# Output weights of layer one kept as halves, and three blocks of layer two split ahead of the seam

## The chip, the cores and the metric

The kernel runs on one core of a Trainium2 chip. TensorE (PE) does the matmuls, VectorE (DVE), ScalarE (ACT) and GpSimd (POOL) the rest, and every DMA is issued by SyncE (SP), on one hardware queue. The metric is the device time in microseconds; the median of three runs of the kernel before is 956.66 us (956.12 to 958.75).

## The reference

Banded causal attention with a distance bias, and on its output two feed-forward layers, all in float32. There are 4 x 576 = 2304 tokens of width 512. The weights come as float64.

```python
scores = where(0 <= rel < 128, q @ k.T / 8 + bias, -1e9)   # 4 batches, 8 heads, 64 wide
x = softmax(scores) @ v                                     # [2304, 512]
g = x @ w_gate; x = (g * sigmoid(g) * (x @ w_val)) @ w_out  # layer one, d_ff 1536
h = x @ w_in
y = (h * tanh(softplus(h))) @ w_out2                        # layer two, d_ff 2048
```

## The kernel before, in words

**Halves.** A float32 operand is split into a high part in the matmul's format (ACT copies it, `hi_act`) and the remainder (DVE subtracts, `lo_dve`). These are its halves. A product of two split operands is three matmuls: high by high, high by low, low by high.

**Weights.** The float64 bits are turned into float32 on the chip by five steps on ACT and DVE (`convert`), and then split (`halves`).

**Attention and layer one** run in five chunks of 384 or 512 tokens (`A_CHUNKS`). While PE does layer one of chunk c, the attention of chunk c+1 is mixed in. The last chunk has no attention beside it. For each of 12 blocks of the hidden width there is a gate and a value group (24 matmuls together, `gv_groups`) and an output group of 12 matmuls (`out_group`). The output weights come in six "rings", r = 0 to 5, each for two output groups, in two SBUF buffers (`ring_tile`). In chunk 0 a ring is converted, its float32 form is written to DRAM (`w1od`, 0.5 MB each) and it is split. In chunks 1 to 4 it is loaded back (`load_ring`, tile `cw`) and split again: one ACT and one DVE instruction on 128x1024 elements. In the last chunk the output groups lag by six, so that groups 5 to 11 stand on PE back to back at its end.

**Layer two** uses seven block products in place of eight. Each of its 16 blocks of input weights (8 used per pass over the tokens, three passes of 768 tokens) is made from a float32 block `w2d` by four differences on POOL (tile `t4`) and a split of seven parts on ACT and DVE (`make_win`, tile `win`, three buffers). Its output weights go through the same steps before the seam (`combos`), and are stored in DRAM as halves (`w2o`). The float32 blocks `w2d` are converted in the stretches of chunks 1 to 3 (`conv_w2`).

**The seam** is the end of the last chunk of layer one and the start of layer two. Behind the last gate and value group PE has output groups 5 to 11, and then `hidden(0, 0)`, `hidden(0, 1)` and so on, 42 matmuls each. `layer2` issues the first loads and the splits of the tokens (`x_parts`) while those output groups run.

**Order.** PE runs in the order in which the code is written (`manual_schedule`). The order on the other engines and on SP is set by the scheduler. Small steps of conversion work wait in a list `bg`, from which `pump` takes some after each PE group. SP issues in order: a DMA that waits for a semaphore holds up all behind it.

Of the kernel before, what the change touches and what calls it, by code (L numbers as in the profile page):

```python
# [27 lines left out]
TB = 384  # L28
NPB = NT // (2 * TB)
NJ = NF2 // 2  # L30

SLOT = {1: 0, 2: 1, 3: 2, 5: 3, 6: 4, 7: 5, 4: 6}
CFG = dict(
# [59 lines left out]
def body(ctx: ExitStack, tc: tile.TileContext, qT, kT, vP, w1, w1o, w2, cst, yT):  # L93
# [7 lines left out]
    ps = ctx.enter_context(tc.tile_pool(name="ps", bufs=4, space=bass.MemoryType.PSUM))  # L101

    x2d = dr.tile([128, CT, NT], F32, name="x2d")
    w1od = dr.tile([NF1 // 2, 128, 1024], F32, name="w1od")
    w2d = dr.tile([NF2, 128, 1024], F32, name="w2d")
    w2o = dr.tile([7, 128, NJ, 2, 256], F32, name="w2o")
    cst_sb = const.tile([128, 452], F32, name="cst_sb")
    nb = {128: cst_sb[:, 0:128], 0: cst_sb[:, 128:256]}
    ident = cst_sb[:, 256:384]
# [298 lines left out]
    def steps(key, fs, front=False):  # L408
        if front:
            bg.extendleft([(key if f is fs[-1] else None, f) for f in fs][::-1])  # L410
            return
        for f in fs[:-1]:
            bg.append((None, f))
        bg.append((key, fs[-1]))
# [36 lines left out]
    def halves(st, alloc, put):  # L451
        def f1():
            st["h"] = alloc()
            hi_act(st["h"][:, 0], st["w"])

        def f2():
            lo_dve(st["h"][:, 1], st["w"], st["h"][:, 0])
            put(st["h"])

        return [f1, f2]  # L460
# [28 lines left out]
    def conv_ring(r):  # L489
        st = {}  # L490

        def spill_it():
            nc.sync.dma_start(out=w1od[r], in_=st["w"])

        def put(w):
            ring[0, r] = w
            stage.pop(("o", r))
            if r + 1 < NF1 // 2:
                stage_other(("o", r + 1), w1o[r + 1])

        steps(
            ("ring", 0, r),
            convert(stage["o", r], st) + [spill_it] + halves(st, ring_tile, put),
        )

    def load_ring(ci, r):
        st = {}

        def f0():
            st["w"] = hp_.tile([128, 1024], F32, tag="cw", name="cw")  # L510
            nc.sync.dma_start(out=st["w"], in_=w1od[r])

        def put(w):
            ring[ci, r] = w

        steps(
            ("ring", ci, r), [f0, lambda: None] + halves(st, ring_tile, put), True
        )

    def conv_w2(blocks, calls):  # L520

        pause = max(6, (calls - 24 - 9 * len(blocks)) // len(blocks))

        def wait(n):
            for _ in range(n):
                bg.append((None, lambda: None))

        def block(i, after):
            st, raw = {}, {}

            def run(k):
                if not raw:
                    raw["f"] = convert(stage.pop(("2", i)), st)
                raw["f"][k]()

            def put():
                nc.sync.dma_start(out=w2d[i], in_=st["w"])

            for k in (0, 2, 3):
                bg.append((None, lambda k=k: run(k)))  # L540
                wait(1)
            if after is not None:
                bg.append((None, lambda: stage_other(("2", after), w2[after])))
            bg.append((None, lambda: run(1)))
            bg.append((None, lambda: run(4)))
            bg.append((None, put))
            wait(pause)

        bg.append((None, lambda: stage_other(("2", blocks[0]), w2[blocks[0]])))
        wait(pause)  # L550
        for i, after in zip(blocks, blocks[1:] + [None]):
            block(i, after)

    def differences(w, x):
        for o, a, b in ((0, w[:, 0], w[:, 1]), (1, w[:, 3], x[:, 0]), (2, w[:, 3], w[:, 0]), (3, x[:, 1], w[:, 2])):
# [247 lines left out]
    def layer2(br):  # L803
# [7 lines left out]
        raws = {}  # L811

        def load_raw(p, j):
            raws[p, j] = br.tile([128, 4, 256], F32, tag="w4", name="w4", bufs=2)
            nc.sync.dma_start(out=raws[p, j], in_=w2d[j].rearrange("p (k n) -> p k n", k=4))

        def make_win(p, j):

            w = raws.pop((p, j))
            x = t4  # L820
            for o, a, b in ((0, w[:, 0], w[:, 1]), (1, w[:, 3], x[:, 0]), (2, w[:, 3], w[:, 0]), (3, x[:, 1], w[:, 2])):
                nc.gpsimd.tensor_tensor(out=x[:, o], in0=a, in1=b, op=ALU.subtract)  # L822
            t = win[p, j] = br.tile([128, 2, 7, 256], F32R, tag="win", name="win")
            for d, src in ((slice(0, 3), w[:, 1:4]), (slice(3, 7), x)):
                hi_act(t[:, 0, d], src)
                lo_dve(t[:, 1, d], src, t[:, 0, d])
# [47 lines left out]
                if i == 7:  # L874
                    add(g[:, 2], g[:, 1], g[:, 0], ALU.subtract)

        load_raw(0, 0)
        t4 = br.tile([128, 4, 256], F32, tag="t4", name="t4", bufs=1)
        xs = x_tiles(br, (7, 5))
        xr = first["x"]  # L880
        xs.update(x_tiles(br, (1, 4, 6, 2, 3)))
        load_raw(0, 1)
        x_parts(xs, xr)
        for j in range(2):
            make_win(0, j)
            load_raw(0, j + 2)
        bp, mish = yield
        yr = yT.rearrange("(c p) t -> p c t", p=128)
        for p in range(NPB):
            loads = [(i, k) for i in ORDER2 for k in range(2)]  # L890
            for j in range(NJ):
                for f, k in ((make_win, p * NJ + j + 2), (load_raw, p * NJ + j + 4)):
                    if k < NPB * NJ:
                        f(*divmod(k, NJ))
                if j >= NJ - 3:
                    load_wout(p, *loads.pop(0))
                hidden(p, j, xs)
# [61 lines left out]
    with tc.manual_schedule(engines={mybir.EngineType.PE}):  # L959
# [28 lines left out]
        while at < lasts[0]:  # L988
            pieces.popleft()[2]()
            at += 1  # L990
            if at == 1:
                conv_w1(0)
                conv_ring(0)
                conv_w1(1)
                nst = len(bg)
                stage_w1(2)
                stage_w1(3)
            f = (at / lasts[0] - CFG["conv_a"]) / (CFG["conv_b"] - CFG["conv_a"])
            while bg and nst - len(bg) < f * nst:
                pump(1)  # L1000
        k = last - 1
        shares = [list(range(i * NF2 // k, (i + 1) * NF2 // k)) for i in range(k)]
        carry = []
        behind += [last_of["act"], last_of["x", 2]]
        for ci, p in enumerate(plansA):
            if ci:
                behind.clear()
            if ci < last:
                win = [pieces.popleft() for _ in range(lasts[ci + 1] - at)]
                at = lasts[ci + 1]  # L1010
            else:
                pump(10000)
                att.__exit__(None, None, None)
                cv = tc.tile_pool(name="cv", bufs=2, side="right", reuse_waits="tile")
                bpool["p"] = cv.__enter__()
                win = []
                for b in range(NJ, NF2):
                    combos(b)
            lag = CFG["lastlag"] if ci == last else 1
            if ci == last:  # L1020
                first["x"] = load_x(xp, 0)
            groups = []
            outs = carry + [out_group(ci, i)[0] for i in range(NF1)]
            for i in range(NF1):
                groups += [("gv", i, f) for f in gv_groups(ci, i)]
                if i < len(carry) or len(outs) > NF1 - 1 - i + lag:
                    groups.append(("o", 0, outs.pop(0)))
            if ci == 0:
                groups[4:6] = groups[5], groups[4]
            carry = outs  # L1030
            total = sum(x[1] for x in win)
            ng = len(groups)
            if 1 <= ci < last:
                own_ = shares[ci - 1]
                conv_w2(own_, CFG["pump_g"] * ng + CFG["pump_p"] * len(win))
            spent = 0.0
            win = collections.deque(win)
            if ci == 0:
                _, cost, e = win.popleft()
                e()  # L1040
                spent += cost
            for gi, (kind, i, f) in enumerate(groups):
                if ci == 0 and kind == "gv" and gi % 3 == 0:
                    if 0 < i < NF1 - 2:
                        conv_w1(i + 2)
                    if i == 0:
                        conv_ring(1)
                        bg.insert(len(bg) - 4, (None, lambda: behind.append(last_of["x", 3])))
                f()
                if ci or not win:  # L1050
                    pump(CFG["pump_g"])
                elif gi % 3 == 0:
                    due = max(1, -(-len(bg) // 4))
                if not ci:
                    pump(due)
                while win and (spent * ng < (gi + 1) * total or gi == len(groups) - 1):
                    _, cost, e = win.popleft()
                    e()
                    spent += cost
                    pump(CFG["pump_p"] if ci else due)  # L1060
# [76 lines left out]
```

## Time and profile before

| | |
|---|---|
| median of the runs | 956.66 us |
| profiled execution, its own time | 955.31 us |
| span of the profile, first to last instruction | 953.4 us |
| PE busy | 924.4 us (97%) |
| DVE / ACT / POOL busy | 702.4 / 524.5 / 204.9 us |
| moved by DMA | 174.86 MB, mean 183 GB/s |

The span leaves 1.9 us of the execution's time around it. A busy PE is one that has matmuls in flight, at whatever clock was granted. What PE misses is found from its idle time and from the stretches in which the granted clock is 0.5 of full.

### The profile page before, as it was taken

The numbers are of one execution on the slowest core, as the hardware profiler recorded it, in microseconds if no ns is written. First come the engines' busy times: TensorE is split into PE (matmuls) and PEld (weight loads), VectorE is DVE, ScalarE is ACT, GpSimd is POOL, SyncE is SP. The second block draws the span as 40 slices with busy tenths as digits, with TensorE's granted clock in tenths as the row PEclk, the third lists the DMA queues.
The fourth block names the chain that finished last, engine by engine and source line by source line (L and its number), as shares of the span: only waits on it lengthen the run. The fifth ranks groups of instructions, "written<-read, shape, count | busy, mean of one in ns | idle before, by whom it ended". The sixth has DMA issues, their size and how long they took to land. (4 is left out here: it accounts for less than half of the span.)

```text
span 953.4 us, 14622 instructions
## 1 busy us (share of the span) xinstructions
PE 924.4 (97%) x5040; PEld 832.0 (87%) x5040; DVE 702.4 (74%) x1341; ACT 524.5 (55%) x1135; POOL 204.9 (21%) x332
## 2 busy tenths in 40 slices
PE   6998999999999999999999998999999999999998
PEld 4766777899988888888889998899999999999997
DVE  6899997687866866567565668788877878677673
ACT  6766667666575655445534445555545555355442
POOL 0314223110210332010113325542012420132000
PEclk9999999999999999999999999999999999999999
DMA  9855434376636554165348993525793257830385
GB/s 305 294 202 197 167 91 126 97 228 198 216 94 202 167 186 134 51 206 168 132 147 284 375 327 101 210 70 193 252 307 110 77 184 261 301 118 4 103 266 183
DMA packets 76921, 174.86 MB, mean 183 GB/s; under 512 B 9136, under 2 KB 52528, under 8 KB 67120
## 3 DMA queue, kind: packets, MB, share of 16 engines
q1 hardware_dynamic: 76848, 173.94, 55.4%
q8 instruction: 40, 0.66, 0.3%
q14 instruction: 33, 0.27, 0.1%
HBM read 138.25 MB, written 35.65 MB: 182 GB/s over the span
## 5 line engine op out<-in xcount | busy, mean ns | idle before, releaser
L114 PE MATMUL g_ps<-xt,w 128*128 128x512 f32 (+1 forms) x1440 | 317.4, 373 | 0.6 <-DVE t L661 0.6
L114 PEld LDWEIGHTS g_ps<-xt,w 128*128 128x128 f32 x1440 | 257.7, 188 | 36.4 <-issue 2.3
L114 PE MATMUL bk<-xs,win 128*128 128x384 f32 x1008 | 180.1, 338 | 5.5 <-DVE G L726 4.9
L114 PEld LDWEIGHTS bk<-xs,win 128*128 128x128 f32 x1008 | 176.0, 189 | 9.2 <-DVE G L726 8.0
L114 PE MATMUL bk<-op,wout 128*128 128x384 f32 x1008 | 175.8, 335 | 0.6 <-DMA wout<-w2o 0.6
L114 PEld LDWEIGHTS bk<-op,wout 128*128 128x128 f32 x1008 | 174.8, 188 | 1.1 <-issue 1.1
L114 PE MATMUL acc<-hh,ring 128*128 128x512 f32 (+1 forms) x480 | 151.6, 379 | 1.9 <-DVE ring L124 1.8
L121 ACT ACTIVATE op<-G 128x768 fp32r<-128x768 f32 x84 | 70.8, 846 | 65.6 <-PE bk L114 63.0
L114 PEld LDWEIGHTS acc<-hh,ring 128*128 128x128 f32 x480 | 91.4, 193 | 15.2 <-DVE ring L124 2.6
L268 POOL TENSOR_SCALAR_AFFINE_SELECT PT<-PT 128x256 f32<-128x256 f32 (+4 forms) x80 | 51.8, 662 | 240.3 <-ACT PT L265 240.1
L124 DVE TENSOR_TENSOR op<-G,op 128x768 fp32r<-128x768 f32 x84 | 79.6, 955 | 26.9 <-ACT op L121 26.3
L822 POOL TENSOR_TENSOR t<-w 128x256 f32<-128x256 f32 x48 | 43.3, 921 | 224.6 <-DVE win L124 206.3
L114 PE MATMUL acc<-hl,ring 128*128 128x512 f32 (+1 forms) x240 | 90.2, 376 | 0.8 <-DVE hl L124 0.8
L237 ACT ACTIVATE Pt<-Pt,sm 128x128 f32<-128x128 f32 (+1 forms) x160 | 62.4, 391 | 17.1 <-DVE sm L233 16.1
L726 DVE TENSOR_TENSOR G<-u,bk 128x384 f32<-128x384 f32 x72 | 39.0, 553 | 31.8 <-PE bk L114 29.7
L121 ACT ACTIVATE hh<-t 128x512 fp32r<-128x512 f32 (+1 forms) x60 | 35.0, 583 | 47.0 <-DVE t L669 46.8
L1081 ACT ACTIVATE G<-G 128x384 f32<-128x384 f32 x72 | 36.8, 519 | 42.2 <-DVE G L726 42.2
L660 ACT ACTIVATE t<-g_ps 128x512 f32<-128x512 f32 (+1 forms) x60 | 32.7, 546 | 45.8 <-PE g_ps L114 45.6
L661 DVE SCALAR_TENSOR_TENSOR t<-t,g_ps 128x512 f32<-128x512 f32 (+1 forms) x60 | 37.6, 626 | 27.0 <-ACT t L660 26.9
L252 ACT ACTIVATE Pt<-Pt,sm 128x128 f32<-128x128 f32 (+1 forms) x144 | 46.3, 391 | 12.4 <-DVE sm L248 12.2
L114 PEld LDWEIGHTS acc<-hl,ring 128*128 128x128 f32 x240 | 46.3, 193 | 6.2 <-DVE hl L124 1.1
L124 DVE TENSOR_TENSOR hl<-t,hh 128x512 fp32r<-128x512 f32 (+1 forms) x60 | 39.8, 663 | 15.2 <-ACT hh L121 14.6
(78 smaller groups left out, 1235.1 us busy)
## 6 DMA issues: line engine op xcount, KB each, us to landing
wout<-w2o SPq DMA_DIRECT2D x42, 1024.0 KB, 6.1
wraw<-w SPq DMA_DIRECT2D x16, 1024.0 KB, 5.8
w2o<-chl SPq DMA_DIRECT2D x16, 896.0 KB, 9.0
wst<-w SPq DMA_DIRECT2D x12, 1024.0 KB, 6.9
cw<-w1od SPq DMA_DIRECT2D x24, 512.0 KB, 4.3
w<-w2d SPq DMA_DIRECT2D x24, 512.0 KB, 3.3
w2d<-cw SPq DMA_DIRECT2D x16, 512.0 KB, 5.0
wraw<-w1o SPq DMA_DIRECT2D x6, 1024.0 KB, 5.1
```

What stands on the lines that cost most here:

```text
L114: nc.tensor.matmul(out=out, lhsT=lhsT, rhs=rhs, start=start, stop=stop, skip_group_check=True)
L121: return nc.scalar.activation(out=out, in_=in_, func=AF.Copy)
L124: return nc.vector.tensor_tensor(out=out, in0=in_, in1=hi.bitcast(F32), op=ALU.subtract)
L237: nc.scalar.activation(out=Pt[:q.qn], in_=Pt[:q.qn], func=AF.Exp, scale=-1.0, bias=sm[:q.qn, i:i + 1], accum_out=sm[:q.qn, 8 + i:9 + i],)
L252: last_of["exp"] = nc.scalar.activation(out=pt, in_=pt, func=AF.Copy, scale=r)
L268: nc.gpsimd.affine_select(out=here, in_=prev, pattern=[[0, m], [1, n]], compare_op=ALU.is_ge, fill=0.0, base=0, channel_multiplier=-1,)
L660: tanhs.append(nc.scalar.activation(out=t[:, :n], in_=st["g"][:, :n], func=AF.Tanh, scale=0.5))
L661: nc.vector.scalar_tensor_tensor(out=t[:, :n], in0=t[:, :n], scalar=1.0, in1=st["g"][:, :n], op0=ALU.add, op1=ALU.mult)
L726: nc.vector.tensor_tensor(out=out, in0=a, in1=b, op=op)
L822: nc.gpsimd.tensor_tensor(out=x[:, o], in0=a, in1=b, op=ALU.subtract)
L1081: nc.scalar.activation(out=out, in_=in_, func=AF.Mish)
```

## The change

It does two things. First, a ring is stored in DRAM as halves (`w1od`, now 1 MB a ring), by chunk 0 after its split, and in chunks 1 to 4 it is loaded straight into its ring buffer; the tile `cw` and the split are gone there. Second, the first `MADE` = 3 blocks of layer two are made (differences and split) in the stretches of chunks 1 to 3, one at the end of each stretch's share (`premade`), and stored as halves (`w2i`, 1.75 MB each). At the seam they are loaded straight into the three `win` buffers; `load_raw` and `make_win` as before begin with block 3, in the first pass only.

```diff
-    w1od = dr.tile([NF1 // 2, 128, 1024], F32, name="w1od")
+    w1od = dr.tile([NF1 // 2, 128, 2, 1024], F32, name="w1od")
+    w2i = dr.tile([MADE, 128, 2, 7, 256], F32, name="w2i")
...
     def load_ring(ci, r):
-            st["w"] = hp_.tile([128, 1024], F32, tag="cw", name="cw")
-            nc.sync.dma_start(out=st["w"], in_=w1od[r])
...
-            ("ring", ci, r), [f0, lambda: None] + halves(st, ring_tile, put), True
+            ring[ci, r] = ring_tile()
+            nc.sync.dma_start(out=ring[ci, r].bitcast(F32), in_=w1od[r])
+        steps(("ring", ci, r), [f0], True)
...
+            if i < MADE:
+                premade(i, st, wait)
...
+    def premade(i, st, wait):
+        def diff():
+            st["x"] = bpool["a"].tile([128, 4, 256], F32, tag="wx", name="wx", bufs=1)
+            st["w4"] = st["w"].rearrange("p (k n) -> p k n", k=4)
+            differences(st["w4"], st["x"])
+        bg.append((None, diff))
+        for part in range(2):
+            def hi(part=part):
+                t = st["t"] = bpool["a"].tile([128, 2, 1024], F32R, tag="wraw", name="wh", bufs=1)
+                st["v"] = t.rearrange("p e (d n) -> p e d n", n=256)[:, :, :4 if part else 3]
+                hi_act(st["v"][:, 0], st["x"] if part else st["w4"][:, 1:4])
+            def lo(part=part):
+                lo_dve(st["v"][:, 1], st["x"] if part else st["w4"][:, 1:4], st["v"][:, 0])
+                d = slice(3, 7) if part else slice(0, 3)
+                nc.sync.dma_start(out=w2i[i, :, :, d], in_=st["v"].bitcast(F32))
...
         def make_win(p, j):
+            if p == 0 and j < MADE:
+                t = win[p, j] = br.tile([128, 2, 7, 256], F32R, tag="win", name="win")
+                nc.sync.dma_start(out=t.bitcast(F32), in_=w2i[j])
+                return
...
-        load_raw(0, 0)
+        make_win(0, 0)
...
-        load_raw(0, 1)
+        make_win(0, 1)
+        make_win(0, 2)
         x_parts(xs, xr)
-        for j in range(2):
-            make_win(0, j)
-            load_raw(0, j + 2)
+        load_raw(0, MADE)
...
-        shares = [list(range(i * NF2 // k, (i + 1) * NF2 // k)) for i in range(k)]
+        shares = [rest_[i * len(rest_) // k:(i + 1) * len(rest_) // k] + [i] for i in range(k)]
```

The order of PE's instructions is the same in both kernels. On SP, before, this stood around the seam, in program order. `w2o` are the last stores of layer two's output weights, `cw` from `w1od` are rings 4 and 5 of the last chunk, and `w4` are the raw blocks of layer two.

```order
L567 DMA cw4_5905<-w2d_74 128x1024
L591 DMA w2o_75<-chl_5804 128x7x256
L511 DMA cw_6063<-w1od_73 128x1024
L591 DMA w2o_75<-chl_5885 128x7x256
L591 DMA w2o_75<-chl_5888 128x7x256
L511 DMA cw_6172<-w1od_73 128x1024
L591 DMA w2o_75<-chl_5928 128x7x256
L591 DMA w2o_75<-chl_5949 128x7x256
L815 DMA w4_6072<-w2d_74 128x1024
L815 DMA w4_6082<-w2d_74 128x1024
L815 DMA w4_6111<-w2d_74 128x1024
L640 DMA x2d_72<-ev_6201 128x2x384
```

In the changed kernel the same place on SP reads as follows (`ring_6037` and `ring_6125` are rings 4 and 5, `win` are blocks 0 to 2).

```order
L509 DMA ring_5943<-w1od_73 128x2048
L610 DMA w2o_75<-chl_5859 128x7x256
L610 DMA w2o_75<-chl_5880 128x7x256
L842 DMA win_6043<-w2i_76 128x3584
L842 DMA win_6053<-w2i_76 128x3584
L842 DMA win_6055<-w2i_76 128x3584
L836 DMA w4_6075<-w2d_74 128x1024
L836 DMA w4_6166<-w2d_74 128x1024
L509 DMA ring_6037<-w1od_73 128x2048
L509 DMA ring_6125<-w1od_73 128x2048
L659 DMA x2d_72<-ev_6151 128x2x384
```

The loads of rings 4 and 5 moved from among the `w2o` stores to behind them and behind five loads of layer two. Each now waits for PE: ring 4 for the end of output group 5, ring 5 for the end of output group 7, whose buffers they take.

On DVE, before, this stood at the seam (`ring` are rings 4 and 5, `win` the splits of blocks 0 to 2, `xs` and `xr` the splits and sums of the tokens).

```order
L124 TENSOR_TENSOR ring_6065<-cw_6063,ring_6065 128x1024
L726 TENSOR_TENSOR xr_5421<-xr_5421 128x2x384
L124 TENSOR_TENSOR win_6106<-w4_6072,win_6106 128x768
L124 TENSOR_TENSOR xs5_6076<-xr_5421,xs5_6076 128x768
L726 TENSOR_TENSOR xr_5421<-xr_5421 128x2x384
L124 TENSOR_TENSOR ring_6174<-cw_6172,ring_6174 128x1024
L124 TENSOR_TENSOR win_6117<-w4_6082,win_6117 128x768
L124 TENSOR_TENSOR xs7_6075<-xr_5421,xs7_6075 128x768
L726 TENSOR_TENSOR xr_5421<-xr_5421 128x2x384
L124 TENSOR_TENSOR win_6106<-t4_6074,win_6106 128x1024
L124 TENSOR_TENSOR xs6_6079<-xr_5421,xs6_6079 128x768
L124 TENSOR_TENSOR win_6220<-w4_6111,win_6220 128x768
```

In the changed kernel DVE has this there (`hl` is the last hidden block of layer one, `ev` its evacuation).

```order
L126 TENSOR_TENSOR hl_6022<-t_6004,hh_6021 128x384
L745 TENSOR_TENSOR xr_5404<-xr_5404 128x2x384 x2
L126 TENSOR_TENSOR xs5_6047<-xr_5404,xs5_6047 128x768
L745 TENSOR_TENSOR xr_5404<-xr_5404 128x2x384
L126 TENSOR_TENSOR xs7_6046<-xr_5404,xs7_6046 128x768
L745 TENSOR_TENSOR xr_5404<-xr_5404 128x2x384
L126 TENSOR_TENSOR xs6_6050<-xr_5404,xs6_6050 128x768
L126 TENSOR_TENSOR xs3_6052<-xr_5404,xs3_6052 128x768
L658 COPY ev_6151<-acc1_5756 128x384
```

The two ring splits and the splits of the first blocks of layer two are gone from between the token splits.

## Rows read from the trace of the kernel before

**Rows 1.** The page: span, and PE and its clock in 40 slices.

```profile
span 953.4 us, 14622 instructions
PE   6998999999999999999999998999999999999998
PEclk9999999999999999999999999999999999999999
```

**Rows 2.** Busy time by stretch: PE, PEld, DVE, ACT, POOL; clock, DMA share, GB/s.

```profile
120.00:560.00 440.00, 437.90 (x2419) 378.56 (x2420) 305.71 (x687) 246.60 (x625) 89.31 (x177) 1.00 0.56 178
520.00:562.00 42.00, 42.00 (x243) 42.00 (x242) 28.26 (x39) 20.67 (x32) 18.83 (x23) 1.00 1.05 371
...
584.03:587.44 3.41, 3.41 (x13) 3.41 (x12) 3.41 (x4) 0.76 (x2) 0.52 (x1) 0.50 0.00 0
597.00:606.00 9.00, 9.00 (x51) 8.52 (x50) 6.46 (x9) 6.38 (x11) 4.04 (x5) 1.00 1.00 401
```

**Rows 3.** Whom PE waited for: us in total, times, longest.

```profile
PE bk L114 <- DVE G L726: 4.9, 9, 2.0
PE acc L114 <- DVE ring L124: 1.8, 1, 1.8
```

**Rows 4.** PE in order of time at the seam: start, us, what, idle before.

```profile
570.01 0.35 PE L114 MATMUL acc<-hh,ring 128*128 128x384 f32 x1
...
583.15 0.62 PE L114 MATMUL acc<-hh,ring 128*128 128x384 f32 x2 [1.80 <-DVE ring L124]
...
588.67 4.35 PE L114 MATMUL bk<-xs,win 128*128 128x384 f32 x24
...
613.55 16.41 PE L114 MATMUL bk<-xs,win 128*128 128x384 f32 x84 [2.00 <-DVE G L726]
...
654.04 6.25 PE L114 MATMUL bk<-op,wout 128*128 128x384 f32 x35
```

**Rows 5.** DVE and POOL at the seam, in order of time.

```profile
581.89 1.21 DVE L124 TENSOR_TENSOR ring<-cw,ring 128x1024 fp32r<-128x1024 f32 x1
593.21 1.23 DVE L124 TENSOR_TENSOR win<-t,win 128x1024 fp32r<-128x1024 f32 x1 [2.76 <-ACT win L121]
...
574.63 2.83 POOL L822 TENSOR_TENSOR t<-w 128x256 f32<-128x256 f32 x2 [14.53 <-DMA w<-w2d]
```

**Rows 6.** PE in order of time, second pass of layer two.

```profile
712.30 20.99 PE L114 MATMUL bk<-xs,win 128*128 128x384 f32 x120
...
772.48 2.79 PE L114 MATMUL bk<-op,wout 128*128 128x384 f32 x15
```

**Rows 7.** SP's issues at the seam, and time to landing of those from 566 to 569.

```profile
562.55 4.34 SPq L591 DMA_DIRECT2D w2o<-chl  x2
566.98 13.64 SPq L815 DMA_DIRECT2D w<-w2d  x3
...
DMA to landing us min/median/max: 7.5/7.9/8.2
```

**Rows 8.** DMA issues of the page: count, KB each, median us to landing.

```profile
w<-w2d SPq DMA_DIRECT2D x24, 512.0 KB, 3.3
...
wraw<-w1o SPq DMA_DIRECT2D x6, 1024.0 KB, 5.1
```

**Rows 9.** Groups of ring and block splits: count, busy, mean ns, idle before.

```profile
L124 DVE TENSOR_TENSOR ring<-cw,ring 128x1024 fp32r<-128x1024 f32 x30 | 37.7, 1257 | 12.3 <-ACT ring L121 11.9 <-DMA v<-vP 0.3
L121 ACT ACTIVATE ring<-cw 128x1024 fp32r<-128x1024 f32 x30 | 31.6, 1053 | 13.7 <-PE acc L114 7.5 <-DMA cw<-w1od 4.4 <-DMA v<-vP 1.4
```

**Rows 10.** PE in order of time: stops of the start and of chunk 0.

```profile
21.63 1.19 PE L259 MATMUL t_ps<-cst_sb,Pt 128*128 128x128 f32 x4 [1.50 <-ACT Pt L252]
...
32.68 0.78 PE L259 MATMUL t_ps<-cst_sb,Pt 128*128 128x128 f32 x4
...
74.17 0.89 PE L259 MATMUL t_ps<-cst_sb,Pt 128*128 128x128 f32 x4 [2.87 <-ACT Pt L252]
...
119.90 0.58 PE L114 MATMUL s_ps<-K,Q 128*128 128x256 f32 x1 [1.53 <-DVE Q L193]
```

More of the change, by code (lines that the diff above doesn't have):

```diff
@@ L30 @@
 NJ = NF2 // 2
+MADE = 3
 SLOT = {1: 0, 2: 1, 3: 2, 5: 3, 6: 4, 7: 5, 4: 6}
@@ L490, in conv_ring @@
         st = {}
-        def spill_it():
-            nc.sync.dma_start(out=w1od[r], in_=st["w"])
         def put(w):
             ring[0, r] = w
+            nc.sync.dma_start(out=w1od[r], in_=w.bitcast(F32))
             stage.pop(("o", r))
@@ L502, in conv_ring @@
             ("ring", 0, r),
-            convert(stage["o", r], st) + [spill_it] + halves(st, ring_tile, put),
+            convert(stage["o", r], st) + halves(st, ring_tile, put),
         )
     def load_ring(ci, r):
-        st = {}
         def f0():
-            st["w"] = hp_.tile([128, 1024], F32, tag="cw", name="cw")
-            nc.sync.dma_start(out=st["w"], in_=w1od[r])
-        def put(w):
-            ring[ci, r] = w
-        steps(
-            ("ring", ci, r), [f0, lambda: None] + halves(st, ring_tile, put), True
-        )
+            ring[ci, r] = ring_tile()
+            nc.sync.dma_start(out=ring[ci, r].bitcast(F32), in_=w1od[r])
+        steps(("ring", ci, r), [f0], True)
     def conv_w2(blocks, calls):
-        pause = max(6, (calls - 24 - 9 * len(blocks)) // len(blocks))
+        pause = max(6, (calls - 7  - 10 * len(blocks) - 22) // (len(blocks) + 1))
         def wait(n):
@@ L552, in conv_w2 @@
             block(i, after)
+    def premade(i, st, wait):
[13 more added lines that the diff above has]
+                nc.sync.dma_start(out=w2i[i, :, :, d], in_=st["v"].bitcast(F32))
+            bg.append((None, hi))
+            wait(1)
+            bg.append((None, lo))
+            wait(5 if part else 10)
     def differences(w, x):
@@ L817, in make_win @@
         def make_win(p, j):
+            if p == 0 and j < MADE:
+                t = win[p, j] = br.tile([128, 2, 7, 256], F32R, tag="win", name="win")
+                nc.sync.dma_start(out=t.bitcast(F32), in_=w2i[j])
+                return
             w = raws.pop((p, j))
@@ L892, in layer2 @@
                 for f, k in ((make_win, p * NJ + j + 2), (load_raw, p * NJ + j + 4)):
-                    if k < NPB * NJ:
+                    if k < NPB * NJ and (f is load_raw or k >= MADE):
                         f(*divmod(k, NJ))
@@ L1000, in body @@
                 pump(1)
+        rest_ = list(range(MADE, NF2))
         k = last - 1
-        shares = [list(range(i * NF2 // k, (i + 1) * NF2 // k)) for i in range(k)]
+        shares = [rest_[i * len(rest_) // k:(i + 1) * len(rest_) // k] + [i] for i in range(k)]
         carry = []
@@ L1047, in body @@
                         conv_ring(1)
-                        bg.insert(len(bg) - 4, (None, lambda: behind.append(last_of["x", 3])))
+                        bg.insert(len(bg) - 3, (None, lambda: behind.append(last_of["x", 3])))
                 f()
```

## The prediction

> **What bounds the kernel now.** I read the page first: PE is the bound, with a busy share of 9 tenths or more in most slices; below that are some of the first four, the last, and slice 25, 572 to 596 us, which is the seam [rows 1]. The table by stretch says the same of the middle: from 120 to 560 us PE is busy 437.9 of 440 us, while DVE is busy 305.7 and ACT 246.6 [rows 2]. So work taken from ACT or DVE there is worth at most the 2.1 us that PE misses. The list of PE's waits, and PE in order of time, then show what the seam costs. PE stops 1.80 us in layer one's last output groups, for the DVE half of a ring [rows 3, 4], and in layer two's first blocks, 2.00 us at 613.55 being the longest of several stops [rows 4]. A stop costs more than itself: just behind the first, the granted clock is 0.50 (1.2 of 2.4 GHz) from 584.03 to 587.44, which loses half of 3.41, 1.7 us [rows 2].
>
> Two durations measure the seam. PE starts output group 5 at 570.01 and layer two at 588.67 [rows 4]. A matmul of 384 columns takes 0.174 us here (120 in 20.99 us in the second pass, the last one's tail included [rows 6]), so the 84 matmuls of groups 5 to 11 need 14.6 of these 18.7 us; the stop and the slow clock are 3.5 of the remaining 4.0. And the first pass needs 65.4 us from 588.67 to its first matmul on output weights at 654.04 [rows 4]; the second pass does the same 336 matmuls in 60.2, from 712.30 to 772.48 [rows 6].
>
> **The change part by part.** The sum is made against the profiled execution, 955.31 us, which is 1.4 us under the median.
>
> *Layer two's first blocks.* Gone from the seam are three times four differences on POOL, two ACT and two DVE splits. They are what layer two waits for there: POOL starts only at 574.63 after a raw block, and DVE has its last split of the second block at 593.21, after PE has begun [rows 5]. With three blocks in their buffers the first pass has three blocks (21.9 us) in which to make the fourth. Its buffer comes free when PE ends block 0, 7.3 us into the pass, and four splits of about 1 us each follow, so it is ready near 12 and due at 21.9. I therefore take the second pass's duration for the first: 65.4 - 60.2 = 5.2 us gained. Bounds: nothing, and 65.4 less 336 x 0.174, which is 7.0.
>
> *The rings in the last chunk.* Here lies the price. Ring 4 is wanted by output group 8, 36 matmuls after 570.01, at 576.3. Before, its float32 form was in `cw` long before, and only the split had to wait for a ring buffer. Now the load itself waits for PE to end group 5 (572.1), and on SP it stands behind the last two `w2o` stores, three `win` loads and two `w4` loads. When do these go? The last stores are issued in a stretch that ends at 566.9, and three raw loads start at 566.98 [rows 7]. The stores wait for splits that stand on DVE behind layer one's own work, so I leave them at that time. The five loads then go right behind, near 567 to 569, before ring 4 can.
>
> What stands ahead in the queue is served first: the raw loads issued there took 7.5 to 8.2 us to land [rows 7], against a median of 3.3 [rows 8]. The difference of 4.6 us at 371 GB/s, the rate of the crowded stretch [rows 2], is 1.7 MB, and the two stores ahead of them are 1.8 MB. The first raw load landed at 574.5, and 0.52 MB of its own take 1.3 us at 401 GB/s, the rate of a stretch of large loads [rows 2]; so all before it was gone at 573.2. From there the new queue is 3 x 1.835 + 2 x 0.524 MB, and ring 4's own 1.05: 7.60 MB, at 401 GB/s 19.0 us. Ring 4 lands at 592.2, and PE stops 15.9 us at 576.3. At 371 GB/s it is 17.4; if ring 4 did not queue at all, 5.1 us for 1 MB on a free queue [rows 8], 0.9 us. I take 15.9, the row of large loads being nearest to these.
>
> The Trainium skill (DMA: Bandwidth & Descriptors, Where 436 GB/s comes from) has it that between HBM and SBUF the HBM side binds at about 358 GB/s for a core; the row above shows 401, so the measurement decides. By the page's figure the queue would take an estimated 21.2 us and the sum would be 2.3 us higher.
>
> Ring 5 lands 2.6 us after ring 4, at 594.8, and PE wants it 24 matmuls (4.2 us) later, so there is no second stop. The stop before the change, 1.8 us, goes: layer one ends 15.9 - 1.8 = 14.1 us later. I leave the clock at one slow period of 1.7 us on both sides. A stop this long isn't in the trace behind the start; there four transposes took 1.19 us at 21.63 and 0.78 at 32.68 [rows 10], so a slow clock can last. If it lasted through all of groups 8 to 11 (48 x 0.174 = 8.4 us), it would cost 6.7 us more. The nearest row is the stop at the same place, so I take nothing more.
>
> *Chunks 1 to 3.* Here 18 of the 24 reloads lose a split of 1.05 us on ACT and 1.26 on DVE [rows 9], and three blocks' differences and splits come in. DMA gains some 18 MB over 440 us, 41 GB/s on top of 178 at a share of 0.56 [rows 2]. All of this lies beside PE's matmuls. Ring loads that wait for PE hold up the loads of q, k and v behind them on SP, which are issued two heads ahead; if that cover failed once, by a stop like the 2.87 us of chunk 0 [rows 10] with its 1.7 of clock, it would cost 4.6 us. I take 0, bounds -2.1 and +4.6.
>
> *Start and chunk 0.* The same instructions run; only their order on ACT and DVE shifts, since the list of background steps is one shorter a ring, and the ring's store is 1 MB. The stops of 2.87 and 1.53 us there [rows 10], each with a slow clock, are worth 4.4 + 3.4 = 7.8 us, and could go or be doubled. I take 0.
>
> The sum is 14.1 - 5.2 = +8.9 us: 964.2 for a profiled execution, 965.6 from the median. I say 965.
>
> **The rivals.** First, *faster: the ring loads are not held up by the five loads ahead.* Ring 4 then lands at 572.1 + 5.1 = 577.2 and PE stops 0.9 us instead of 1.8. With layer two's 5.2 us the kernel gains 6.1: 950.6. It decides from a stop below 7.0 us (5.2 + 1.8), that is when ring 4 lands before 583.3. For it: nothing in PE's order has changed and 5.1 us is the row for 1 MB. Against it: the landings of [rows 7]. The Trainium skill (DMA: Bandwidth & Descriptors, Queues, rings and completion order) says both that a DMA engine consumes a ring's descriptors in order and that completion is not first in, first out per issuing engine; the landings agree with the first, and the second would be this rival.
>
> Second, *no change: the shuffled order takes away the stops of chunk 0*, 7.8 us against the 8.9: 957.8. For it: DVE's order there does change. Against it: its work there is the same.
>
> Third, *worse: the clock stays low after the long stop*, +6.7: 972. For it: the slow transposes of the start; against it: behind the stop at the same place the slow stretch is 3.41 us [rows 2].
>
> That the change doesn't do what it says isn't likely: by the same rates the three blocks land at 577.8, 582.4 and 586.9, before PE could want them.
>
> **How the numbers follow.** Forecast 0.70, first rival 0.13, second 0.07, third 0.10. About 0.3% (2.9 us) is what a measurement of this kernel can tell from no change. The forecast's own range is 961 to 969, from 371 GB/s on one side and 7.0 us gained in layer two on the other, with a microsecond or two from chunks 0 to 3. Leaving out the first rival below and a little above, the range is 956 to 973. Faster is the first rival, 0.13; same is the second and a small edge of the forecast, 0.09; slower is the rest, 0.78.
>
> **What would show it.** In the changed profile PE should have one long stop before a matmul `acc<-hh,ring`, put down to the DMA `ring<-w1od`, near 576 and 14 to 17 us long, with DMA at a share near 1.0 in that time; layer two should start near 602, and its first pass take 60 to 61 us with no stop over 1 us. I am wrong if that stop is below 7 us, if the ring's load lands while the `win` loads are still under way, or if the time moves before 560 us instead.

## The result, and the profile after

The changed kernel takes 970.9 us (median; 968.88 to 972.29), the kernel before 957.01 in the same comparison (956.12 to 958.75). The ratio is 1.014, with a 95% interval of 1.0122 to 1.0159: slower by about 14 us. The profiled executions are 970.52 and 955.31 us, their spans 968.8 and 953.4.

First, whom PE waited for in the changed kernel (us in total, times, longest); it answers to [rows 3].

```profile
PE acc L116 <- DMA ring<-w1od: 14.7, 1, 14.7
...
PE o_ps L116 <- issue: 4.4, 2, 2.4
PE s_ps L116 <- DVE Q L195: 3.2, 3, 1.6
PE bk L116 <- DVE G L745: 2.7, 8, 0.5
```

The stop on the DVE half of a ring is gone, and one on a ring's load, eight times as long, is there. PE in order of time at the seam, to hold against [rows 4, 6]:

```profile
600.36 0.66 PE L116 MATMUL acc<-hh,ring 128*128 128x384 f32 x1 [14.67 <-DMA ring<-w1od]
...
610.48 20.99 PE L116 MATMUL bk<-xs,win 128*128 128x384 f32 x120
632.00 14.86 PE L116 MATMUL bk<-xs,win 128*128 128x384 f32 x84 [0.53 <-DVE G L745]
647.07 14.86 PE L116 MATMUL bk<-xs,win 128*128 128x384 f32 x84 [0.21 <-DVE G L745]
...
670.60 29.65 PE L116 MATMUL bk<-op,wout 128*128 128x384 f32 x170
```

Layer two's first pass, 610.48 to 670.60, now takes 60.1 us instead of 65.4. SP's issues at the seam, and below them the time to landing of the two ring loads, answer to [rows 7]:

```profile
576.19 3.03 SPq L842 DMA_DIRECT2D win<-w2i  x3
579.27 1.32 SPq L836 DMA_DIRECT2D w<-w2d  x2
581.55 4.48 SPq L509 DMA_DIRECT2D ring<-w1od  x2
```

```profile
DMA to landing us min/median/max: 17.0/17.8/18.7
```

The first ring load was issued at 581.55, a microsecond behind the last of five loads. Those five landed 10.4 to 17.2 us after their issue, the last by 597.8, and the ring load 18.7 us after its own, at 600.2, when PE goes on. The table by stretch (columns as in [rows 2]) shows what filled that time, and what the clock did behind the stop:

```profile
520.00:562.00 42.00, 42.00 (x240) 41.50 (x239) 26.35 (x38) 18.35 (x30) 16.94 (x23) 1.00 1.05 370
580.00:600.00 20.00, 5.69 (x33) 5.37 (x31) 10.32 (x13) 5.35 (x8) 2.81 (x4) 0.76 1.01 424
600.40:604.10 3.70, 3.70 (x12) 3.70 (x13) 0.00 (x0) 0.00 (x0) 0.00 (x0) 0.50 0.10 40
221.80:225.20 3.40, 3.40 (x18) 3.07 (x14) 3.30 (x7) 2.45 (x10) 0.00 (x0) 0.50 0.99 398
331.10:334.40 3.30, 3.30 (x25) 2.87 (x26) 3.24 (x17) 3.20 (x12) 0.10 (x1) 0.50 0.94 359
```

The DMA engines are full from 580 to 600, at 424 GB/s. But the last two rows are from 222 and 331 us, long before the seam, and they too have the clock at half. So I took the start of every matmul in both timelines, paired them by their order on PE, and read the lag of the changed kernel: -0.1 us at 139 us of the kernel before, **9.2** at 575, just ahead of the stop, 21.8 at 588, where layer two begins, 16.5 at 633 and 15.6 at the end. Nine of the sixteen microseconds are lost in the stretches with attention. The three longest new stops there, PE in order of time; first the kernel before at the place of the first of them, then the changed kernel:

```profile
217.83 1.74 PE L114 MATMUL o_ps<-PT,v 128*64 128x256 f32 x20
```

```profile
220.54 2.06 PE L116 MATMUL o_ps<-PT,v 128*64 128x256 f32 x20 [2.35 <-issue]
...
241.82 0.39 PE L116 MATMUL s_ps<-K,Q 128*128 128x256 f32 x1 [1.36 <-DVE Q L195]
...
331.00 3.26 PE L116 MATMUL o_ps<-PT,v 128*64 128x256 f32 x24 [2.02 <-issue]
```

The stops of 2.35, 1.36 and 2.02 us and the half clock of 3.4 us behind the first and the third, of which half is lost, come to 9.1 us. DVE and ACT ahead of the first of these, and the issues on SP of what they wait for:

```profile
216.01 0.69 DVE L436 TENSOR_SCALAR cw<-wraw 128x1024 int32<-128x1024 int32 x1 [4.53 <-DMA wraw<-w]
...
218.22 0.42 DVE L221 COPY_PREDICATED s_ps<-cst_sb,s_ps 128x256 f32<-128x256 uint8 x1
...
219.89 0.55 DVE L680 SCALAR_TENSOR_TENSOR t<-t,g_ps 128x384 f32<-128x384 f32 x1
```

```profile
216.01 1.16 ACT L424 ACTIVATE cg<-wraw 128x1024 bf16<-128x1024 bf16 x1 [4.33 <-DMA wraw<-w]
```

```profile
205.88 2.00 SPq L509 DMA_DIRECT2D ring<-w1od  x1
207.99 0.37 SPq L478 DMA_DIRECT2D wraw<-w  x1
```

Both engines stand on the staged raw words of a layer two block, which are converted for later use. Behind that step, in DVE's order, stand the softmax mask of a score tile (L221), more conversion steps, and a step of layer one's gate (`t<-t,g_ps`). PE goes on at 220.54, just behind the end of the gate step at 220.44. The view names no releaser for this stop ("issue"), so that PE waits for the gate step is read from the times; the stop at 331.00 fits too, where the same gate step ends at 330.90. (The Trainium skill, Perfetto Trace Analysis, Tensor Engine Instruction, calls the queues of ACT and DVE strictly first in, first out; these rows agree: the mask starts only when the step on the words has run.) For the stop at 241.82 the releaser is named, Q, and again a step on the words stands ahead of it on DVE:

```profile
237.07 0.69 DVE L436 TENSOR_SCALAR cw<-wraw 128x1024 int32<-128x1024 int32 x1 [2.42 <-DMA wraw<-w]
...
241.08 0.69 DVE L195 SCALAR_TENSOR_TENSOR Q<-qraw,Q 64x512 fp32r<-64x512 f32 x1
```

Over the whole run the waits on the staged words are these, before and then changed:

```profile
ACT cg L422 <- DMA wraw<-w: 37.6, 16, 7.3
```

```profile
ACT cg L424 <- DMA wraw<-w: 24.2, 11, 4.3
...
DVE cw L436 <- DMA wraw<-w: 23.7, 11, 4.5
```

Before, ACT stood longer and DVE not at all, and PE missed only 2.1 us from 120 to 560 us [rows 2]. So the length of such a wait says little by itself; which engine stands, and what is queued behind it, says more.

### The profile page after: what moved, and what is told of

Its sections match the earlier page's. It is cut to its first block, busy times and chain, and to the rows that moved or that the text cites. A ratio compares the mean times of both kernels' runs of the same rounds, so it can differ in the third digit from the quotient of the medians.

```text
span 968.8 us, 14539 instructions
## 1 busy us (share of the span) xinstructions
PE 924.6 (95%) x5040; PEld 833.5 (86%) x5040; DVE 670.7 (69%) x1317; ACT 503.3 (52%) x1111; POOL 187.3 (19%) x332
## 4 chain that ended last, share of the span: by engine, by line
PE 73%; DVE 11%; DMA 9%; issue 3%; ACT 3%; SPq 1%; DVEq 0%; ACTq 0%; POOL 0%
PE bk L116 33%; PE g_ps L116 23%; PE acc L116 12%; DMA wraw<-w 3%; PE s_ps L116 2%; PE o_ps L116 2%; DMA ring<-w1od 2%; DVE G L745 1%; DVE cw L441 1%; DVE cw L447 1%; PE t_ps L261 1%; DVE Pt L235 1%; SPq L178 1%; DMA w2d<-cw 1%; DVE cw L436 1%
## 5 line engine op out<-in xcount | busy, mean ns | idle before, releaser
L116 PE MATMUL bk<-xs,win 128*128 128x384 f32 x1008 | 177.6, 335 | 2.7 <-DVE G L745 2.7
L116 PE MATMUL acc<-hh,ring 128*128 128x512 f32 (+1 forms) x480 | 151.4, 378 | 14.7 <-DMA ring<-w1od 14.7
L116 PEld LDWEIGHTS acc<-hh,ring 128*128 128x128 f32 x480 | 91.2, 192 | 27.5 <-issue 15.5
L126 DVE TENSOR_TENSOR op<-G,op 128x768 fp32r<-128x768 f32 x84 | 79.6, 955 | 27.1 <-ACT op L123 26.6
L270 POOL TENSOR_SCALAR_AFFINE_SELECT PT<-PT 128x256 f32<-128x256 f32 (+4 forms) x80 | 42.9, 552 | 236.3 <-ACT PT L267 236.2
L847 POOL TENSOR_TENSOR t<-w 128x256 f32<-128x256 f32 x42 | 35.3, 860 | 247.2 <-DVE win L126 221.1
L680 DVE SCALAR_TENSOR_TENSOR t<-t,g_ps 128x512 f32<-128x512 f32 (+1 forms) x60 | 37.8, 629 | 50.0 <-ACT t L679 50.0
L688 DVE SCALAR_TENSOR_TENSOR t<-t,g_ps 128x512 f32<-128x512 f32 (+1 forms) x60 | 37.7, 629 | 25.6 <-PE g_ps L116 24.9
```

The costliest lines, as they stand in the source:

```text
L116: nc.tensor.matmul(out=out, lhsT=lhsT, rhs=rhs, start=start, stop=stop, skip_group_check=True)
L126: return nc.vector.tensor_tensor(out=out, in0=in_, in1=hi.bitcast(F32), op=ALU.subtract)
L270: nc.gpsimd.affine_select(out=here, in_=prev, pattern=[[0, m], [1, n]], compare_op=ALU.is_ge, fill=0.0, base=0, channel_multiplier=-1,)
L680: nc.vector.scalar_tensor_tensor(out=t[:, :n], in0=t[:, :n], scalar=1.0, in1=st["g"][:, :n], op0=ALU.add, op1=ALU.mult)
L688: nc.vector.scalar_tensor_tensor(out=t[:, :n], in0=t[:, :n], scalar=0.5, in1=vps[:, :n], op0=ALU.mult, op1=ALU.mult)
```

## The experiments

The lags below are read as above, in us, at 139, 575, 588, 633 us and the end of the kernel before. "Rings alone" and the like are the kernel before with that part of the change; each time has the kernel before from its own comparison beside it. A lag is read from one profiled execution of each kernel, and executions differ: rings alone was profiled at 969.09 us, kernel 8 at 968.23 and kernel 10 at 970.64, each the slowest of its runs (from 961.04, 961.10 and 964.66 on). So two lags that are a few microseconds apart are not told apart.

| kernel | us (before) | ratio, 95% | lag at 139, 575, 588, 633, end |
|---|---|---|---|
| the change | 970.9 (957.0) | 1.0122 to 1.0159 | -0.1, 9.2, 21.8, 16.5, 15.6 |
| 1 rings alone | 964.1 (956.2) | 1.0047 to 1.0095 | -0.2, 14.0, 11.2, 13.9, 14.0 |
| 2 blocks alone | 953.7 (956.2) | 0.9961 to 0.9996 | 1.0, 2.3, -1.1, -2.2, -2.2 |
| 3 ring loads first | 964.9 (956.2) | 1.0066 to 1.0112 | -0.8, 12.0, 8.9, 12.3, 11.6 |
| 4 one block made | 963.8, one run | - | -0.9, 10.8, 14.4, 9.1, 8.8 |
| 5 blocks, raw earlier | 950.2 (956.5) | 0.9921 to 0.9948 | -0.8, 1.5, -1.0, -5.0, -5.1 |
| 6 rings, four turns | 961.2 (956.5) | 1.0039 to 1.0072 | -3.2, 6.1, 6.3, 5.7, 6.1 |
| 7 rings, half the bytes | 962.3 (956.5) | 1.0047 to 1.0089 | -0.9, 9.8, 5.8, 7.0, 7.2 |
| 8 rings, cw held | 964.2 (957.0) | 1.0041 to 1.0098 | -0.6, 13.8, 16.7, 13.1, 13.2 |
| 9 rings, staged once | 954.1 (957.0) | 0.9948 to 0.9988 | -0.2, 1.4, -1.1, 0.4, 0.5 |
| 10 rings, split back | 967.3 (957.2) | 1.0066 to 1.0129 | -0.3, 11.6, 14.1, 15.7, 15.5 |
| 11 rings, two staged | 973.1 (956.6) | 1.0160 to 1.0196 | 8.7, 17.3, 15.2, 16.8, 17.1 |
| 12 before, early tile | 960.0 (957.2) | 1.0013 to 1.0043 | 2.4, 5.8, 8.5, 5.5, 5.5 |

**1 and 2: the two parts, each alone.**

```diff
 # 1: conv_ring and load_ring of the change; the blocks of layer two as before
+            ring[ci, r] = ring_tile()
+            nc.sync.dma_start(out=ring[ci, r].bitcast(F32), in_=w1od[r])
...
 # 2: premade and make_win of the change; w1od, conv_ring and load_ring as before
+                nc.sync.dma_start(out=t.bitcast(F32), in_=w2i[j])
```

> Rings as halves alone; the blocks of layer two as before. The changed kernel lost 9.3 us ahead of the seam, 12.6 us at layer one's end, and won 5.3 us in layer two's first pass. Theory (rings: the 1 MB ring loads push the staging loads of w2 back in the one queue, and ACT and DVE, in order, stand on them): PE still reaches output group 8 some 8 to 10 us late. At the seam two raw blocks (1.05 MB) and not 6.55 MB stand ahead of ring 4: a stop of about 2 us, first pass 65 us. Time 964 to 967. Rival (blocks: the premade differences and splits cause the stops ahead of the seam): PE reaches group 8 within 2 us of before, time 956 to 959.

> The three premade blocks alone; rings as 0.5 MB in float32, split after each load, as before. Theory (rings cause the lag ahead of the seam): PE reaches output group 8 within 2 us of before, no stop on a ring's DMA, first pass of layer two 60 to 61 us; with the ring's split no longer behind block splits on DVE the stop of 1.8 us and its slow clock go too: 948 to 952. Rival (blocks cause the lag): 8 to 10 us late at group 8, 957 to 961.

Of rings alone, PE's waits:

```profile
PE s_ps L114 <- DVE Q L193: 7.5, 4, 4.7
PE bk L114 <- DVE ev L630: 5.4, 1, 5.4
...
PE o_ps L114 <- issue: 3.4, 2, 2.0
...
PE acc L114 <- DMA ring<-w1od: 1.0, 1, 1.0
```

Without the blocks' loads ahead of it the ring load costs 1.0 us, yet the lag ahead of the seam is there as in the change: 14.0 at 575, in an execution 5 us above the median. So the loss in the stretches comes with the rings. (The 5.4 us on `ev` are a stop in layer two's first blocks.) Blocks alone are slightly faster than before, though short of the 948 to 952 us expected, and have 2.3 us of lag there. What they still lose is at the seam:

```profile
PE bk L116 <- ACT u L813: 3.0, 1, 3.0
```

ACT ahead of that stop, in order of time:

```profile
596.58 0.85 ACT L123 ACTIVATE win<-w 128x768 fp32r<-128x768 f32 x1 [1.43 <-DMA w<-w2d]
600.29 1.06 ACT L123 ACTIVATE win<-t 128x1024 fp32r<-128x1024 f32 x1 [2.86 <-POOL t L856]
601.25 0.51 ACT L1115 ACTIVATE G<-G 128x384 f32<-128x384 f32 x1
601.66 0.47 ACT L813 ACTIVATE u<-bk 128x384 f32<-128x384 f32 x1
```

The raw words of block 3 were issued behind all three blocks and landed at 596.5; ACT stands on their split with the output that PE needs, `u`, behind it.

**3 and 4: the queue at the seam.**

```diff
 # 3: the change, with the ring loads of the last chunk ahead
+        with tc.issue_after(ring_dma[0].ins):
+            for j in range(MADE):
+                make_win(0, j)
+            load_raw(0, MADE)
...
 # 4: the change, with one block made ahead; blocks 1 and 2 loaded raw and split as before
-MADE = 3
+MADE = 1
...
```

> The changed kernel with its win loads and first raw loads put on SP behind rings 4 and 5 instead of ahead of them; nothing else moved. Queue theory: ring 4 lands about 5 us after its issue instead of 18.7, PE's stop before group 8 falls from 14.7 to 0 to 2 us, the three blocks still land in time, first pass 60 to 61 us; the lag of 9 us ahead of the seam stays: 955 to 959. Rival (a 1 MB ring load is slow by itself, or its late issue alone makes the stop): the stop stays above 7 us, 963 or more.

> The changed kernel with one premade block instead of three: ahead of ring 4 stand 1.84 + 1.05 MB instead of 5.5 + 1.05. Queue theory: 3.67 MB less at 4.3 us for 1.835 MB, so ring 4 lands 8.6 us earlier and the stop is 6.1 us (5 to 8). Rival (ring load slow by itself or by its issue): 14 to 15 us as with three.

Ring loads put first land 4.7 us after their issue, and PE's stop on them is 0.7 us; with fewer bytes ahead (4) it is 5.6. The stop follows the bytes in the queue. But the time of 3 came out at 964.9, not 955 to 959: the lag of the stretches stayed (12.0 at 575), and a new stop took the old one's place, on ACT at block 3's split, whose words now landed at 610.3:

```profile
PE bk L116 <- ACT u L806: 5.4, 1, 5.4
...
PE bk L116 <- DMA win<-w2i: 1.1, 1, 1.1
```

**5: blocks alone, with one load earlier.**

```diff
         make_win(0, 0)
+        load_raw(0, MADE)
...
         x_parts(xs, xr)
-        load_raw(0, MADE)
```

> The premade blocks alone (ring tiles reloaded as before), with one load moved: the raw words of block 3 are issued behind the first block's halves instead of behind all three. Theory: with the premade blocks alone PE stood 3.0 us at about 602 us on an ACT step queued behind block 3's split, whose raw words landed last (596.5 us), and the low clock after that stop (603.3 to 606.8) cost about 1.7 us more; both go, so the time falls from 953.7 to 949 to 951.5 us and the stop on ACT is under 0.6 us. Rival: the halves of block 2, now 1.3 us later in the same queue (about 596.5 us), become the stop: a wait on the DMA of win at about 598 us of 1 to 3 us, and the time stays at 952 to 955 us.

950.2 us: 0.65% faster than before (0.52 to 0.79%), 20.7 us under the changed kernel by the medians, the fastest of all. PE in order of time, its first pass:

```profile
587.65 20.99 PE L116 MATMUL bk<-xs,win 128*128 128x384 f32 x120
608.86 5.48 PE L116 MATMUL bk<-xs,win 128*128 128x384 f32 x30 [0.22 <-DVE G L754]
614.64 9.81 PE L116 MATMUL bk<-xs,win 128*128 128x384 f32 x54 [0.30 <-ACT u L813]
```

No stop at block 3, and no slow clock from 575 to 640 us. The rival's wait on block 2's halves isn't there.

**6 to 8: what brought the lag, by bytes, turns or buffer.**

```diff
 # 6: rings alone
-        steps(("ring", ci, r), [f0], True)
+        steps(("ring", ci, r), [f0] + [lambda: None] * 3, True)
 # 7: rings alone; TensorE reads index 0 for index 1 in chunks 1 to 3
-            nc.sync.dma_start(out=ring[ci, r].bitcast(F32), in_=w1od[r])
+            nc.sync.dma_start(out=ring[ci, r][:, 0].bitcast(F32), in_=w1od[r, :, 0])
 # 8: rings alone; two small copies in cw as steps 3 and 4
+            st["w"] = hp_.tile([128, 1024], F32, tag="cw", name="cw")
+            nc.sync.dma_start(out=st["w"][:, 0:128], in_=w1od[r, :, 0, 0:128])
...
```

> Ring tiles as halves alone (the kernel that took 964.14 us), but each reload takes four turns of the background list again (three empty ones behind the load), as in the kernel before, so that the conversion of layer two's weights keeps the spacing it had. Theory A, bytes: the staging load of the next raw block stands behind a 1 MB ring load on the one queue whatever the spacing, and ACT and DVE stand on it; then PE's lag ahead of the seam stays at 9 to 15 us and the time at 961 to 966 us, with DVE waits on the staged words of 3 to 5 us. Theory B, spacing: the three turns that fell away brought the conversion forward to before its data; then the lag falls to 0 to 4 us and the time to 952 to 957 us.

> Ring tiles as halves alone, but a reload in chunks 1 to 3 brings only the high halves (0.5 MB, as many bytes as in the kernel before), and TensorE reads them in place of the low ones too: what is left out is the low halves' contribution of layer one's output weights in those chunks. TensorE's instructions are the same in number and order. Theory A, bytes: the lag ahead of the seam falls to 0 to 4 us, and the time to 951 to 957 us. Theory B, spacing: the conversion still comes three turns earlier, the lag stays at 9 to 15 us and the time at 961 to 966 us.

> Ring tiles as halves alone (964.14 us), but each reload also holds one of the two cw buffers for four turns of the background list, as the reload of the kernel before did: a 64 KB load into it, one small copy on ACT and one on DVE stand in for the split. Neither fewer bytes nor more turns brought the time back, so what is left is the order on DVE. Theory C: with the cw buffer free, DVE's step that reads the staged raw words is put ahead of softmax steps and stands there until the words land; held again, that step comes later, DVE's wait on the staged words goes (under 8 us in all), the lag ahead of the seam falls to 0 to 4 us and the time to 953 to 958 us. Rival D: it is the time that the split itself filled on ACT and DVE; then nothing changes, 960 to 966 us with 20 us or more of DVE waits on the staged words.

None gave the time back. From 139 to 575 us the lag grew by 9.3 (6), 10.7 (7) and 14.4 us (8), against 14.2 for rings alone. Kernel 6 has its four turns back and lags, against theory B, though its 6.1 at 575 is under theory A's 9 too; 7 has half the bytes of the ring loads and lags, against theory A. Kernel 8 changed DVE's order in part: its waits on the words fell to 13.1 us (27.1 in rings alone), between the bounds of theory C and rival D, and it waits 15.7 us for ACT's first step. But ACT stands on the words all the same, once for 9.0 us, and there DVE stands 8.3 us with it; ACT's waits in kernel 8:

```profile
ACT cg L422 <- DMA wraw<-w: 34.0, 14, 9.0
```

Each of the three falls as the single cause.

**9: without the staging loads.**

```diff
-                bg.append((None, lambda: stage_other(("2", after), w2[after])))
+                bg.append((None, lambda: stage.update({("2", after): once[0]})))
```

> Ring tiles as halves alone, but layer two's raw weights are staged once and that one block is converted 16 times: what is left out is the values of the other 15 blocks and their 1 MB staging loads. The conversions and PE's instructions are the same in number. If PE's lag ahead of the seam comes from ACT and DVE standing on the staged words with softmax steps behind them, it falls to -2 to 3 us, the stops on o_ps and on Q fall under 5 us together, and the time to 950 to 956 us. Rival: if it comes from something else that the halves changed (the order of the conversions among themselves, the ring loads' hold on the queue), the lag stays at 8 us or more and the time at 959 us or more.

PE's waits in it:

```profile
PE bk L114 <- DVE ev L638: 5.1, 1, 5.1
PE s_ps L114 <- DVE Q L193: 4.1, 3, 2.2
...
PE acc L114 <- DMA ring<-w1od: 1.3, 1, 1.3
```

The lag at 575 is 1.4 instead of 14.0, the stop on `o_ps` is gone, and the time 954.1 us. So without the staging loads nearly all of the loss in the stretches is gone. That it is the waits on them, and not the 15 loads of 1 MB that this run leaves out, is not shown by it; kernel 7, which moves some 9 MB less in the same stretches and lags, speaks against the bytes.

**10 to 12: three tries at the cause.**

```diff
 # 10: rings alone; high halves into the ring tile, low halves through cw
+            hi_act(st["w"], st["w"])
+            nc.vector.tensor_tensor(out=st["h"][:, 1], in0=st["w"], in1=st["w"], op=ALU.max)
...
 # 11: rings alone; a block's words staged a block ahead
-        stage[key] = bpool["a"].tile([128, 2048], I32, tag="wraw", name="wraw", bufs=1)
+        stage[key] = bpool["a"].tile([128, 2048], I32, tag="wraw", name="wraw", bufs=2)
...
 # 12: the kernel before; the ring tile taken at the load
+            st["t"] = ring_tile()
+            nc.sync.dma_start(out=st["t"][:, 1, 0:128].bitcast(F32), in_=w1od[r, :, 0:128])
...
```

> Ring tiles as halves alone (964.14 us) with as many bytes per reload, but the work of the split put back: the high halves are loaded into the ring tile, the low ones into a cw buffer, which ACT copies in place (128x1024) and DVE writes into the ring tile (128x1024), in four turns, as the split of the kernel before took them. Bytes, turns and the buffer alone have each been tried. If the work of the split on ACT and DVE was what kept the conversions of layer two's weights behind their data, the lag ahead of the seam falls to 0 to 5 us and the time to 953 to 959 us, though ACT and DVE have more to do. Rival: it is a matter of which order the engines happen to get, and the split counts for nothing by itself: 960 to 968 us, with a lag of 8 us or more.

> Ring tiles as halves alone (964.14 us), but the raw words of layer two are staged in two tiles, each load issued a whole block of conversions ahead; to make room ACT's scratch tile goes from two to one, softmax tiles from 10 to 8 and its sums from 8 to 6. Nothing is left out. If ACT and DVE standing on the staged words is what costs, ACT's and DVE's waits on them fall from 29 to 32 us each to under 6 us together, PE's lag ahead of the seam from 15 to 0 to 4 us, and the time to 952 to 957 us. Rival: the kernel without staging loads was faster because 15 MB fewer were moved; then the waits go and the lag stays at 8 us or more, 959 us or more.

> The kernel before with one thing of the halves taken over: a reload takes its ring tile at the load instead of at the split (a 64 KB load into the tile, ahead of the usual load into the cw buffer, stands for the direct load; the split overwrites it), so that SP waits for TensorE's release of that tile as it does where the halves are loaded straight in. Bytes, turns, buffers and splits are those of before. Theory E (the risk that the forecast named and priced at -2.1 to +4.6 us): SP standing on the ring tile, with staging, query and key loads behind it, is what makes the staged words late; then the time rises to 961 to 966 us, SP's wait on TensorE for the ring tile is 20 us or more and the lag ahead of the seam 5 us or more. Rival: SP's long stands on that tile (up to 19 us, at 460 to 510 us in the kernels with halves) lie where nothing that the next conversion needs is behind them; then the time stays at 955 to 959 us and the lag under 4 us, and what shifted is the order that the engines got.

The split put back (10) restores nothing. Kernel 11 doesn't answer its question: it lags by 8.7 us at 139 us already, where rings alone do not, so its changed buffers cost time of their own, and the loads, though listed a block ahead, still ended ACT's waits (up to 4.3 us). In 12 SP does stand for the ring tile, but for a third of the 56.6 us (longest 19.0) of rings alone, and PE stops 5.1 us on a ring's split:

```profile
SPq L511 <- PE acc L114: 18.7, 6, 5.3
```

```profile
587.67 1.01 PE L114 MATMUL acc<-hh,ring 128*128 128x384 f32 x2 [5.08 <-DVE ring L124]
```

It is 0.28% slower (0.13 to 0.43%), between the two expectations: the lag is 5.8 at 575, over theory E's 5, but 2.4 of it was there at 139, and it grew by only 3.4 us in the stretches. So the early tile as tried here brings back a part at most; what SP's longer stands in the kernels with halves cost is not settled by it.

## Why the prediction was right, and where it was not

The forecast was 965 us in a range of 956 to 973, and slower was named likeliest; 970.9 lies in the range. But it lies outside the forecast's own 961 to 969. The range reaches to 973 because it takes in the third rival, a lasting slow clock (972), which did not come; what filled that room is a loss that the sum put at 0. That much is luck. And one of the prediction's own signs of being wrong came true in part: 9.2 us of the time moved before 560 us. Its steps:

*The queue at the seam* held. Five loads stand ahead of ring 4 on SP, and the DMA engines serve them first: stop 14.7 us, forecast 15.9; ring 5 lands 2.5 us later (18.7 and 17.0 us after issues 4.17 us apart), forecast 2.6. The loads land in the order of their issue. The Trainium skill (DMA: Bandwidth & Descriptors, Queues, rings and completion order) has it that a DMA engine consumes a ring's descriptors in order; the trace agrees. The first rival would have left a stop under 7 us. Kernels 3 and 4 show the cause: the stop is 0.7 us with none of the five ahead and 5.6 with fewer bytes. The rate in the stretch was 424 GB/s where I took 401. The 358 that the Trainium skill (DMA: Bandwidth & Descriptors, Where 436 GB/s comes from) gives for loads from HBM is again not what binds here. The loads went out at 576 to 580 us instead of 567 to 569, together with PE, which was 9 us late; the stop kept its size because both moved, which the forecast did not foresee. It began at 585.7 and not near 576, and layer two at 610.5 and not near 602.

*The clock* behind that stop: half speed for 3.70 us, some 1.9 us lost, where I took 1.7. The third rival, a clock that stays low through groups 8 to 11, did not come: the clock is full again at 604.1, six microseconds before they end. Its rows, the slow transposes of the start, were durations alone; for 21.60 to 22.80 us of the kernel before the view gives a granted clock of 1.00.

*Layer two's first pass* held: 60.1 us against a forecast of 60.2, no stop over 0.53.

So layer one's end, 14.1 by the sum, was 21.8 - 9.2 = 12.6, and the pass gave back 5.3.

*Chunks 1 to 3* is the step that was mis-sized. I took 0 with an upper bound of 4.6; they cost 9.3, twice the bound. I let only one stop on a held load into it, and weighed the work on ACT and DVE by its sum, which did fall (DVE is busy 282 of 440 us there, where [rows 2] has 306; the DMA rate rose by 31 GB/s, from 178 to 209, where I took 41). By the rows above, not sums but order cost the time: a conversion step that reads words still in flight stands on an engine ahead of steps that PE waits for. Two of the three stops also bring a slow clock, of 3.4 us each. By the lag at the end the change costs 15.6 us (13.9 by the medians) where the sum had 8.9: 9.3 more here, 1.5 less at layer one's end, 0.9 given back after 633 us.

What stays open is which feature of the rings moves the conversions into that position. Bytes, turns, the cw buffer and the split were each tried alone, and none is the cause by itself. The early tile alone cost 0.28%, with 3.4 us of lag in the stretches, but with a third of SP's wait in rings alone, so SP's stands behind the ring loads, the risk that the prediction named and priced at 4.6 us at most, stay a possible cause. All kernels that load halves and stage their words lose 8 to 15 us between 139 and 575 us. Their waits on the words are split differently between the engines (in kernel 10 DVE does not wait for them at all, and it lags too); why the orders of before and of the blocks alone cost nothing like it, these runs don't tell.

## What to carry to other kernels

A load that waits for a buffer is late twice: once for the buffer, and once for every byte that was issued on the queue in the meantime; price it by the bytes ahead, and then ask what becomes last when it is moved ahead of them. When a change takes work off engines that aren't the bound, look not at their sums but at which of their steps wait for a transfer and what stands behind those steps. And try the parts of a change alone: one half of this one, with a single load moved, is 0.65% faster than the kernel before, while the whole is 1.4% slower.

## What the runs showed of the hardware

Behind a stop of PE the granted clock is at half (1.2 of 2.4 GHz) for a time that does not follow the stop's length. In the change it is 3.70 us behind 14.67 us at the seam and 3.4 us behind 2.35 and 2.02; before, 3.41 us behind 1.80 [rows 2]. In rings alone the clock falls within a stop of 5.39 us, and of the 6.83 us at half in this row the 4.26 in which PE is busy lie behind it. Behind the stop of 1.36 us at 241.82 in the change there is none: from 242 to 245 us the granted clock is 1.00.

```profile
603.92:610.75 6.83, 4.26 (x13) 4.29 (x14) 2.93 (x4) 2.90 (x5) 2.82 (x4) 0.50 0.50 163
```

And loads of 0.5 to 1.8 MB on one queue moved 424 GB/s over 20 us, from 580 to 600 us in the changed kernel, while PE stood for 14.3 of them.
